# Output stores of 32 full rows, and a second product that takes its last inputs late in two of its four groups

## The chip, the cores and the metric

The kernel runs on one core of one Trainium2 chip. The metric is the device time of one execution in microseconds (us); the time of a kernel is the median of its runs.

## The reference

Three stages follow each other, all in float32 (the two feed-forward parts get their weights as float64 and convert them on the chip).

```python
# attention without softmax: q, k, v are 8 x 8 x 576 x 64 (batch, head, token, feature)
kv  = einsum('bhsd,bhse->bhde', k, v)
out = einsum('bhsd,bhde->bhse', q, kv)
out = out / sqrt(mean(out*out, axis=-1) + 1e-6) * g_norm
x   = out.transpose(0, 2, 1, 3).reshape(4608, 512)
# first feed-forward, 512 -> 768 -> 512
h = maximum(maximum(x @ w1, x @ w2), x @ w3)
x = h @ w_out
# second feed-forward, 512 -> 2048 -> 512
r = maximum(x @ w_in, 0)
y = (s * r*r + b) @ w_out2          # 4608 x 512
```

## The kernel before

Activations lie transposed, features on the 128 partitions and tokens along a row. Each float32 matrix product is made of three products of two halves (`mm3`: high by high, high by low, low by high); a half is split off by ScalarE (ACT, a rounding copy, line 91) and VectorE (DVE) or GpSimd (POOL, a subtraction, line 92).

**Order.** All steps are put on a list with a position (`at(pos, fn, ...)`) and traced in the order of their positions by `run`. TensorE (PE) and SyncE (SP, which issues every DMA of the kernel before) keep that order; DVE, ACT and POOL are ordered by a scheduler that works with estimated times, so their order can shift when an estimate does. A DMA waits, on SP, for its data, its buffer and the DMA eight places earlier in a rotation of eight semaphores; whatever stands behind it on SP waits too.

**Stage one, attention and first feed-forward** (to about 755 us). For each of nine token batches j, 18 groups `g1` (three weights by six blocks m of 128 hidden features) are computed while attention of the next batch is prepared. The maximum over three weights gives `h`, which `h_split` splits into a pair `h_m`. Then come four output groups `g2` (n = 0 to 3): `g2_mm` adds up 18 matmuls, three for each of `h_0` to `h_5`, in one PSUM bank; `g2_out` copies the bank and stores it to DRAM (`x1d`). In a batch after the first, group n stands at position t + 18 + n, its matmuls in the order m = 0 to 5.

**Stage two, input product of the second feed-forward** (about 755 to 1116 us), with a seven-product scheme (Winograd's) for 2 x 2 blocks.

**Stage three, output product** (about 1116 us to the end). Ten passes H = 0 to 9, two for each of five token groups; the last token group has half the width, so passes 8 and 9 take half the time. In each pass `z_load` brings operands from DRAM (`z<-gd`), `z_right` adds and splits them into six rotating `zx` pairs, `z_product` multiplies (product i of seven, four steps each, six matmuls a step), `z_combine` adds up on DVE. After each odd pass `put` turns the result: `o` is one of four rotating 128 x 512 buffers (`stage2`), DVE transposes 32 x 32 blocks into it (line 720), SP stores it. Buffer `o` number 5 can be written when the stores of number 1 have landed. In `o`, partition 32a + r at place (b, f) holds row 32b + r of 128 token rows, feature 128a + f. For pass pairs of full width there are eight `o` (32 stores of 64 KB, line 725), for the last pair four (32 stores of 32 KB, line 729). On SP the stores of a pair stand ahead of the `z_load`s of the pass after next; those for the next pass are out already, except for the last pass.

Of the kernel before, what the change touches and what calls it, by code (L numbers as in the profile page):

```python
# [8 lines left out]
F32 = mybir.dt.float32  # L9
F32R = mybir.dt.float32r  # L10
# [9 lines left out]
P = 128  # L20
N = 512
# [7 lines left out]
def attention_max_ffn_relu2_ffn(ctx: ExitStack, tc, q, k, v, g_norm, w1, w2, w3, wo, wi, w2o, s, b, out):  # L29
# [13 lines left out]
    nc = tc.nc  # L43
    B, H, S, D = q.shape
# [5 lines left out]
    M1 = DF1 // P  # L50
    M2 = DF2 // P
    REM = S - N
# [3 lines left out]
    G1 = 3 * M1  # L56
# [7 lines left out]
    def at(pos, fn, *args):  # L64
        plan.append((pos, len(plan), fn, args))
# [11 lines left out]
    base = ctx.enter_context(tc.tile_pool(name="base", bufs=1))  # L77
# [19 lines left out]
        nc.tensor.matmul(ps, lhsT=w[:, 1, sl], rhs=xh, start=False, stop=last)  # L97

    nc.scalar.preload_act_table_set("natural_log_exp_and_others")
    onesf = base.tile([P, P], F32, name="onesf")  # L100
    nc.vector.memset(onesf, 0.0)
    for h in range(2):
        nc.vector.memset(onesf[h * D:(h + 1) * D, h * D:(h + 1) * D], 1.0 / D)
    ones = base.tile([P, P], F32R, name="ones")
    nc.vector.tensor_copy(out=ones, in_=onesf)
    eps = base.tile([P, 1], F32, name="eps")
    nc.vector.memset(eps, EPS)
    g_sb = base.tile([P, 1], F32, name="g_sb")
# [17 lines left out]
    actx = ExitStack()  # L126
    at_ = actx.enter_context(tc.tile_pool(name="attn", bufs=1))
    psa = actx.enter_context(tc.tile_pool(name="psa", bufs=1, space=PSUM))

    kvf = at_.tile([P, NP, P], F32, name="kvf")  # L130
    nc.gpsimd.memset(kvf, 0.0)
# [172 lines left out]
    def o_sq(bb, p, src):  # L304
        sq = st["sq", p] = at_.tile([P, N], F32, tag="sq", name=f"sq_{bb}_{p}")
        act(out=sq, in_=src, func=AF.Square)
# [82 lines left out]
    def plan_kv(bb, load, mm):  # L389
        at(mm(0) - 2.9 * US, load_rem, bb)  # L390
        for p in range(NP):
            at(load(p), load_kv, bb, p)
            at(mm(p), kv_mm, bb, p)
        at(mm(NP - 1) + 1.2 * US, kv_out, bb)

    def plan_norm(bb, p, t, u):

        if bb:
            at(t + u, sq_split, bb, p)
        at(t + 3.3 * u, ms_mm, bb, p)  # L400
        at(t + 4 * u, ms_ln, bb, p)
        at(t + 6 * u, ms_newton, bb, p)
# [22 lines left out]
    for p in range(NP):  # L425
        a = 6.5 + 3.4 * p
# [15 lines left out]
    for j in range(NB):  # L442
        t = SL * j
        if j + 1 < B:
            bb = j + 1
            xpb = 3 if j else 2
            if bb < 4:
                kt = us(4 + 15 * bb)
                plan_kv(bb, lambda p: kt + (2 * p - 3.9) * US, lambda p: kt + 2 * p * US)
            else:  # L450
                plan_kv(bb, lambda p: t - 4 + p - 1.9, lambda p: t - 4 + p + 0.5)
            at(max(t - 10, us(20)), load_q, bb, 0, NP)
            at(t + 0.2, kv_diag, bb)
            for p in range(NP):
                a = t + 3 * p
                at(a + 0.4, q_turn, bb, p)
                if bb:
                    at(a + 1.3, q_split, bb, p)
                at(a + 3.5, o_mm, bb, p)
                at(a + 4.3, o_out, bb, p)  # L460
                plan_norm(bb, p, a + 4.5, 0.9)
                at(t + G1 + 0.2 + 0.5 * p, x_split, bb, p, nc.gpsimd if p < xpb else nc.vector)
            at(t + 13.3, o_rems, bb)
        elif j + 1 == B:
            for p in range(NP):
                a = t + 3 * p

                def sq(p=p):
                    st["o", B, p] = o_rem[:, p, :]
                    o_sq(B, p, o_rem[:, p, :])  # L470

                at(a + 0.4, sq)
                plan_norm(B, p, a + 0.5, 0.9)
                at(t + G1 + 0.2 + 0.5 * p, x_split, B, p, nc.gpsimd if p < 3 else nc.vector)
        for g in range(G1):
            if j or g >= 4:
                at(t + g, g1_part, j, g, range(KD))
            at(t + max(g, j == 0 and 3 or 0) + 1.01, g1_out, j, g)
            if g % 3 == 2:
                at(t + max(g, j == 0 and 3 or 0) + 1.25, h_split, j, g // 3)  # L480
        for n in range(KD):
            if j:
                at(t + G1 + max(n, 0.3), g2_mm, j, n, range(M1))
            at(t + G1 + n + 1.01 if j else t + G1 + 3 + 0.3 * n, g2_out, j, n)
        if not j:
            for m in range(M1):
                for n in range(KD):
                    at(t + G1 + 0.3 + m * 0.5 + 0.01 * n, g2_mm, j, n, [m])
# [12 lines left out]
    NQ = B // 2 + 1  # L501
# [23 lines left out]
    def stage2(nm):  # L525
        turn[0] += 1
        return base.tile([P, N], F32, tag=("t", "st")[turn[0] % 2], bufs=2, name=nm)
# [187 lines left out]
    def put(H, c, u):  # L715

        qq = H // 2
        o = stage2(f"o_{H}_{c}_{u}").rearrange("p (b f) -> p b f", b=4)
        for m in range(4):
            nc.vector.transpose(o[:, :, 32 * m:32 * m + 32], p2["o"][c][:, m, u * P:(u + 1) * P])  # L720
        for a in range(4):
            f, part = slice(a * P, (a + 1) * P), slice(32 * a, 32 * a + 32)
            if qq < NQ - 1:
                r0 = (2 * qq + c) * S + u * P
                nc.sync.dma_start(out=out[r0:r0 + P, f].rearrange("(b r) f -> r b f", r=32), in_=o[part])
            else:
                for e in range(2):
                    r0 = (4 * c + 2 * u + e) * S + N
                    nc.sync.dma_start(out=out[r0:r0 + REM, f].rearrange("(b r) f -> r b f", r=32),
                                      in_=o[part, 2 * e:2 * e + 2])  # L730

# [30 lines left out]
    for H in range(2 * NQ):  # L764
        t = T4 + 14 * H
        for i in range(7):
            for kk in range(4):
                at(t + 2 * i + 0.5 * kk - 2.4, z_right, H, i, kk)
                at(t + 2 * i + 0.5 * kk, z_product, H, i, kk)
            at(t + 2 * i + 1.9, z_combine, H, i)  # L770
        for i, free in ((0, 2), (1, 3), (4, 4), (5, 5), (6, 6)):
            for u in range(4 if i == 1 else 2):
                first = {0: -5.8, 1: (-3.8, -3.7, -1.8, 0.15)[u], 4: -4.8, 6: -3.8, 5: -2.8}[i]
                at(t + first if H == 0 else t - 14 + 2 * free - 2.4 + 1.55 + 0.01 * u, z_load, H, i, u)
        if H % 2:
            for c in range(2):
                for u in range(width(H // 2) // P):
                    at(t + 12.4 + 2 * c + 0.4 * u, put, H, c, u)
# [27 lines left out]
```

## Time and profile before

| | us |
|---|---|
| runs, median of 3 | 1494.72 (1493.74 to 1497.67) |
| profiled execution, time | 1489.72 |
| profiled execution, span | 1487.8 |
| TensorE busy (94%) | 1397.1 |
| VectorE busy (66%) | 985.7 |
| ScalarE busy (53%) | 784.2 |
| GpSimd busy (35%) | 524.9 |

The span is the profiled execution from its first to its last instruction. Busy shares are averages over three stages; waits are read stage by stage. PE's matmuls overlap, so the distance of two starts (0.23 us for 512 columns) is the measure of its pace and not the duration of one.

### The profile page before, as it was taken

To read this page: it belongs to the slowest core of one execution; us is meant where nothing else is said; L and a number is where in the kernel's file an instruction comes from. 1 tells how busy PE (TensorE), PEld (TensorE's weight loads), DVE (VectorE), ACT (ScalarE), POOL (GpSimd) and SP (SyncE) were. 2 spreads that over 40 slices of the span, in tenths; PEclk is the share of its full clock that TensorE was granted. 3 is DMA by queue.
4 is the path that set the end of the run, shared out by engine and by line. 5 is a ranking of instruction groups with operands and counts; after the bars stand their busy time and mean duration, and the time that the engine had idled before them with its cause. 6 is when DMAs were issued, how large, how long until landed. Compare 5 with 4: busy or idle time off the path is not lost.

```text
span 1487.8 us, 19756 instructions
## 1 busy us (share of the span) xinstructions
PE 1397.1 (94%) x6820; PEld 1143.4 (77%) x6820; DVE 985.7 (66%) x1561; ACT 784.2 (53%) x1393; POOL 524.9 (35%) x381
## 2 busy tenths in 40 slices
PE   5777899999999999999999999899998999999995
PEld 2565687878787878787878788887786888888895
DVE  4999564736363737354475746747887888988885
ACT  4545453535343535333366757766786555555553
POOL 3666443434353525331102223222433414141412
PEclk9889999999999999999999999999999999999998
DMA  9974242536374732313125344352667463646342
GB/s 199 196 192 82 85 74 92 104 127 104 107 110 120 111 108 56 86 36 113 46 106 204 138 165 165 124 194 114 219 225 243 127 201 114 214 136 178 120 133 66
DMA packets 232340, 198.44 MB, mean 133 GB/s; under 512 B 128176, under 2 KB 183472, under 8 KB 230576
## 3 DMA queue, kind: packets, MB, share of 16 engines
q1 hardware_dynamic: 232240, 197.19, 47.8%
q8 instruction: 53, 0.87, 0.3%
q14 instruction: 47, 0.39, 0.1%
HBM read 122.68 MB, written 74.45 MB: 133 GB/s over the span
## 4 chain that ended last, share of the span: by engine, by line
PE 36%; DVE 6%; issue 5%; DMA 4%; ACT 2%; POOL 2%; SPq 0%; DVEq 0%; POOLq 0%; ACTq 0%
PE zs_a L693 12%; PE ps_a L625 6%; PE zs_b L693 6%; PE zs_c L693 3%; PE ps_b L625 3%; PE g L96 1%; PE g L97 1%; PE g L95 1%; PE ps_c L625 1%; DVE cs L530 1%; DMA xl<-x1d 1%; DMA z<-gd 1%; DVE zx L92 1%; POOL d L530 1%; DVE x_q L92 1%
## 5 line engine op out<-in xcount | busy, mean ns | idle before, releaser
L95 PE MATMUL g<-xh,w_w 128*128 128x512 f32 x648 | 259.0, 403 | 5.4 <-ACT xh L91 5.4
L96 PE MATMUL g<-xl,w_w 128*128 128x512 f32 x648 | 258.7, 399 | 0.0
L97 PE MATMUL g<-xh,w_w 128*128 128x512 f32 x648 | 256.9, 397 | 0.0
L91 ACT ACTIVATE zx<-z 128x512 fp32r<-128x512 f32 (+1 forms) x280 | 162.0, 588 | 148.8 <-PE zs_a L693 56.3
L625 PE MATMUL ps_a<-x_q,w_q 128*128 128x512 f32 (+1 forms) x960 | 210.1, 370 | 11.3 <-DVE cs L530 8.4
L693 PE MATMUL zs_a<-zx,w_q 128*128 128x512 f32 (+1 forms) x960 | 203.2, 369 | 0.0
L625 PEld LDWEIGHTS ps_a<-x_q,w_q 128*128 128x128 f32 x960 | 167.4, 188 | 46.0 <-DVE cs L530 11.7
L92 DVE TENSOR_TENSOR zx<-z,zx 128x512 fp32r<-128x512 f32 (+1 forms) x234 | 172.2, 754 | 36.4 <-ACT zx L91 35.9
L693 PEld LDWEIGHTS zs_a<-zx,w_q 128*128 128x128 f32 x960 | 168.7, 189 | 30.4
L530 POOL TENSOR_TENSOR d<-cs,r 128x512 f32<-128x512 f32 (+1 forms) x40 | 59.8, 1503 | 282.7 <-ACT r L646 227.3
L95 PEld LDWEIGHTS g<-xh,w_w 128*128 128x128 f32 x648 | 123.7, 191 | 33.3 <-ACT xh L91 7.1
L97 PEld LDWEIGHTS g<-xh,w_w 128*128 128x128 f32 x648 | 124.4, 192 | 27.9 <-issue 0.5
L96 PEld LDWEIGHTS g<-xl,w_w 128*128 128x128 f32 x648 | 124.5, 192 | 26.5 <-DVE xl L92 0.4
L92 POOL TENSOR_TENSOR zx<-z,zx 128x512 fp32r<-128x512 f32 (+1 forms) x46 | 60.0, 1303 | 210.8 <-ACT zx L91 210.8
L167 POOL TENSOR_TENSOR tr_ctr<-tr_ctr 128x512 int32<-128x512 int32 x42 | 55.9, 1330 | 191.1 <-ACT tr_ctr L160 186.8
L369 DVE TENSOR_TENSOR h<-g,h 128x512 f32<-128x512 f32 x108 | 73.9, 684 | 57.7 <-PE g L97 57.6
L693 PE MATMUL zs_b<-zx,w_q 128*128 128x512 f32 (+1 forms) x480 | 105.6, 374 | 5.2 <-DVE zx L92 4.5
L625 PE MATMUL ps_b<-x_q,w_q 128*128 128x512 f32 (+1 forms) x480 | 105.5, 368 | 0.6 <-ACT cs L635 0.5
L693 PEld LDWEIGHTS zs_b<-zx,w_q 128*128 128x128 f32 x480 | 84.6, 191 | 23.0 <-DVE zx L92 6.8
L625 PEld LDWEIGHTS ps_b<-x_q,w_q 128*128 128x128 f32 x480 | 84.2, 188 | 16.1 <-ACT cs L635 1.0
L96 PE MATMUL g<-h,w_o 128*128 128x512 f32 x216 | 85.6, 396 | 10.1 <-DVE h L92 10.1
L95 PE MATMUL g<-h,w_o 128*128 128x512 f32 x216 | 86.5, 400 | 6.3 <-ACT w_o L91 4.2
(156 smaller groups left out, 2433.4 us busy)
## 6 DMA issues: line engine op xcount, KB each, us to landing
z<-gd SPq DMA_DIRECT2D x64, 512.0 KB, 4.4
gd<-cs SPq DMA_DIRECT2D x96, 256.0 KB, 2.0
z<-gd SPq DMA_DIRECT2D x48, 256.0 KB, 4.1
x1d<-x SPq DMA_DIRECT2D x36, 256.0 KB, 2.8
k<-in_k_dram SPq DMA_DIRECT2D x32, 256.0 KB, 4.7
v<-in_v_dram SPq DMA_DIRECT2D x32, 256.0 KB, 5.1
raw_craw<-in_moe_w_in_dram SPq DMA_DIRECT2D x16, 512.0 KB, 4.2
wd<-tr_ctr SPq DMA_DIRECT2D x32, 256.0 KB, 2.9
```

The costliest lines, as they stand in the source:

```text
L91: act(out=hi, in_=src, func=AF.Copy)
L92: eng.tensor_tensor(out=lo, in0=src, in1=hi.bitcast(F32), op=ALU.subtract)
L95: nc.tensor.matmul(ps, lhsT=w[:, 0, sl], rhs=xh, start=first, stop=False)
L96: nc.tensor.matmul(ps, lhsT=w[:, 0, sl], rhs=xl, start=False, stop=False)
L97: nc.tensor.matmul(ps, lhsT=w[:, 1, sl], rhs=xh, start=False, stop=last)
L167: nc.gpsimd.tensor_tensor(out=t, in0=t, in1=r, op=ALU.add)
L369: nc.vector.tensor_tensor(out=st["h", m], in0=ps, in1=st["h", m], op=ALU.max)
L530: eng.tensor_tensor(out=out, in0=in0, in1=in1, op=op)
L625: nc.tensor.matmul(ps, lhsT=w[:, a, c], rhs=x[:, b_, :n], start=new and k == 0 and e == 0, stop=k == HK - 1 and e == 2, skip_group_check=True)
L693: nc.tensor.matmul(ps, lhsT=w[:, a, c], rhs=x[:, b_, :n], start=new and k_ == 0 and e == 0, stop=k_ == 3 and e == 2, skip_group_check=True)
```

## The change

**The stores.** A store now takes one place b of `o`: 32 token rows with all 512 features, from all 128 partitions, to one closed piece of 64 KB in DRAM. The DRAM side is written as 4 feature blocks of 32 rows of 128 features, the SBUF side as 128 partitions of 128 features. Number and size stay the same for the full-width pairs (32 of 64 KB); the last pair has 16 of 64 KB where it had 32 of 32 KB, and four of these, those with odd j of the second half c = 1, are issued by ACT.

**The second product.** In batches 1 to 8, groups n = 0 and n = 1 first take `h_0` to `h_4`, and then both take `h_5`; groups 2 and 3 are as before. `g2_out` of group 0 moves from position 1.01 to 2.01 after the start of the groups, that of group 1 from 2.01 to 2.11.

**Constants.** `onesf` and `ones` move from the pool that lasts to the pool of the attention stage.

```diff
         for n in range(KD):
             if j:
-                at(t + G1 + max(n, 0.3), g2_mm, j, n, range(M1))
-            at(t + G1 + n + 1.01 if j else t + G1 + 3 + 0.3 * n, g2_out, j, n)
+                if n < 2:
+                    at(t + G1 + max(n, 0.3), g2_mm, j, n, range(M1 - 1))
+                    at(t + G1 + 1.8 + 0.01 * n, g2_mm, j, n, [M1 - 1])
+                else:
+                    at(t + G1 + n, g2_mm, j, n, range(M1))
+            at(t + G1 + max(n + 1.01, 2.01 + 0.1 * n) if j else t + G1 + 3 + 0.3 * n, g2_out, j, n)
...
-        for a in range(4):
-            f, part = slice(a * P, (a + 1) * P), slice(32 * a, 32 * a + 32)
+        for j in range(4):
             if qq < NQ - 1:
-                r0 = (2 * qq + c) * S + u * P
-                nc.sync.dma_start(out=out[r0:r0 + P, f].rearrange("(b r) f -> r b f", r=32), in_=o[part])
+                r0 = (2 * qq + c) * S + u * P + 32 * j
             else:
-                for e in range(2):
-                    r0 = (4 * c + 2 * u + e) * S + N
-                    nc.sync.dma_start(out=out[r0:r0 + REM, f].rearrange("(b r) f -> r b f", r=32),
-                                      in_=o[part, 2 * e:2 * e + 2])
+                r0 = (4 * c + 2 * u + j // 2) * S + N + 32 * (j % 2)
+            eng = nc.scalar if qq == NQ - 1 and c and j % 2 else nc.sync
+            eng.dma_start(out=out[r0:r0 + 32].rearrange("r (a f) -> a r f", a=4), in_=o[:, j])
```

On PE, where the second product of batch 1 begins (`g_1_0` and `g_1_1` are its first two groups), the order before is:

```order
L95 MATMUL g_1_0_1821<-h_4_1757,w_o_1185 128x512
L96 MATMUL g_1_0_1821<-h_4_1757,w_o_1185 128x512
L97 MATMUL g_1_0_1821<-h_4_1757,w_o_1185 128x512
L95 MATMUL g_1_0_1821<-h_5_1818,w_o_1237 128x512
L96 MATMUL g_1_0_1821<-h_5_1818,w_o_1237 128x512
L97 MATMUL g_1_0_1821<-h_5_1818,w_o_1237 128x512
L95 MATMUL g_1_1_1845<-h_0_1438,w_o_1007 128x512
```

Now the rows with `h_5` of the first group stand behind 15 matmuls of the second:

```order
L97 MATMUL g_1_1_1842<-h_4_1757,w_o_1185 128x512
L95 MATMUL g_1_0_1821<-h_5_1818,w_o_1237 128x512
L96 MATMUL g_1_0_1821<-h_5_1818,w_o_1237 128x512
L97 MATMUL g_1_0_1821<-h_5_1818,w_o_1237 128x512
L95 MATMUL g_1_1_1842<-h_5_1818,w_o_1237 128x512
L96 MATMUL g_1_1_1842<-h_5_1818,w_o_1237 128x512
L97 MATMUL g_1_1_1842<-h_5_1818,w_o_1237 128x512
```

Both groups end later by that, and the third begins at the same place as before.

On DVE, in the first steps of pass 8 (`o_1_1` to `o_1_3` are the sixth to eighth `o` of the pair before it), the order before is:

```order
L720 STREAM_TRANSPOSE o_1_1_12205<-xlo_11552 128x4x32 x4
L530 TENSOR_TENSOR z_2_11955<-z_2_11955,z_0_1_11903 128x256
L530 TENSOR_TENSOR z_3_11957<-z_3_11957,z_0_1_11903 128x256
L530 TENSOR_TENSOR z_0_11951<-z_0_11951,z_5_0_12043 128x256
L530 TENSOR_TENSOR z_1_11953<-z_1_11953,z_5_0_12043 128x256
L720 STREAM_TRANSPOSE o_1_2_12223<-xlo_11552 128x4x32 x4
L92 TENSOR_TENSOR zx_12276<-z_2_11955,zx_12276 128x256
L92 TENSOR_TENSOR zx_12286<-z_3_11957,zx_12286 128x256
L720 STREAM_TRANSPOSE o_1_3_12238<-xlo_11552 128x4x32 x4
```

Now more of pass 8's own work stands between the last two `o`:

```order
L724 STREAM_TRANSPOSE o_1_2_12223<-xlo_11552 128x4x32 x4
L92 TENSOR_TENSOR zx_12314<-z_1_11953,zx_12314 128x256
L534 TENSOR_TENSOR z_3_11957<-z_3_11957,z_5_1_12045 128x256
L92 TENSOR_TENSOR zx_12324<-z_2_11955,zx_12324 128x256
L92 TENSOR_TENSOR zx_12351<-z_4_0_12001,zx_12351 128x256
L92 TENSOR_TENSOR zx_12364<-z_4_0_12001,zx_12364 128x256
L92 TENSOR_TENSOR zx_12373<-z_4_1_12003,zx_12373 128x256
L724 STREAM_TRANSPOSE o_1_3_12238<-xlo_11552 128x4x32 x4
```

The transposes moved back by about five DVE instructions; after the earlier pairs they moved back by two to four.

On SP, at the end of the program, before:

```order
L670 DMA z_6_1_12473<-gd_97 128x2x256
L729 DMA out_dram<-o_0_0_12781 32x2x128 x8
L729 DMA out_dram<-o_0_1_12800 32x2x128 x8
L729 DMA out_dram<-o_1_0_12827 32x2x128 x8
L729 DMA out_dram<-o_1_1_12840 32x2x128 x8
```

and now, with two more of each of the last two on ACT:

```order
L674 DMA z_6_1_12473<-gd_91 128x2x256
L731 DMA out_dram<-o_0_0_12781 4x32x128 x4
L731 DMA out_dram<-o_0_1_12796 4x32x128 x4
L731 DMA out_dram<-o_1_0_12819 4x32x128 x2
L731 DMA out_dram<-o_1_1_12828 4x32x128 x2
```

The shape is that of the DRAM side, its outermost size first: 32 before, 4 now. 32 issues on SP became 12, and 4 on ACT.

## Rows read from the trace of the kernel before

**Rows 1.** Waits of PE over the span: total us, times, longest us
```profile
PE g L96 <- DVE h L92: 10.1, 7, 2.4
```

**Rows 2.** Stretches: us, busy (count) of PE, PEld, DVE, ACT, POOL; PEclk, DMA share, GB/s
```profile
200.00:752.00 552.00, 541.91 (x2647) 442.08 (x2646) 294.20 (x430) 231.61 (x402) 204.22 (x144) 1.00 0.39 93
...
1196.00:1221.00 25.00, 25.00 (x112) 20.71 (x111) 24.62 (x56) 14.53 (x25) 4.19 (x3) 1.00 0.59 167
1221.00:1233.00 12.00, 12.00 (x55) 9.93 (x54) 7.16 (x11) 5.45 (x10) 1.98 (x2) 1.00 0.78 253
...
1428.00:1444.00 16.00, 15.87 (x121) 15.08 (x120) 14.40 (x49) 9.30 (x26) 3.31 (x4) 1.00 0.50 127
1445.00:1451.00 6.00, 6.00 (x52) 6.00 (x52) 4.18 (x12) 3.58 (x9) 0.74 (x1) 1.00 0.84 238
```

**Rows 3.** PE in order of time, batches 1 and 2: start us, us, line, tile [idle before]
```profile
225.91 0.39 PE L95 MATMUL g<-h,w_o 128*128 128x512 f32 x1
227.45 0.50 PE L96 MATMUL g<-h,w_o 128*128 128x512 f32 x1 [1.15 <-DVE h L92]
228.02 0.39 PE L95 MATMUL g<-h,w_o 128*128 128x512 f32 x1
228.71 0.39 PE L95 MATMUL g<-h,w_o 128*128 128x512 f32 x1
...
301.22 0.50 PE L96 MATMUL g<-h,w_o 128*128 128x512 f32 x1 [2.39 <-DVE h L92]
```

**Rows 4.** SP in order of time, behind pass 7 and at the end
```profile
1428.03 16.71 SPq L725 DMA_DIRECT2D out_dram<-o  x32
1444.84 0.94 SPq L670 DMA_DIRECT2D z<-gd  x2
...
1470.57 14.90 SPq L729 DMA_DIRECT2D out_dram<-o  x32
```

**Rows 5.** First split of pass 9 on ACT and DVE, and PE at its start
```profile
1447.82 0.42 ACT L91 ACTIVATE zx<-z 128x256 fp32r<-128x256 f32 x1 [0.29 <-PE zs_c L693]
1448.30 5.92 PE L693 MATMUL zs_a<-zx,w_q 128*128 128x256 f32 x48
1448.48 0.42 DVE L92 TENSOR_TENSOR zx<-z,zx 128x256 fp32r<-128x256 f32 x1
```

**Rows 6.** Stores, full-width pairs and last: issue ns min/median/max; landing of the last's
```profile
L725 SPq DMA_DIRECT2D out_dram<-o x128: 315/444/2125, 1199.8 to 1443.2; - x128
...
L729 SPq DMA_DIRECT2D out_dram<-o x32: 343/425/427, 1470.6 to 1485.0; - x32
...
DMA to landing us min/median/max: 1.5/1.6/1.6
```

**Rows 7.** Issues of weight loads with unequal sides (512 pieces onto 128 partitions of 4)
```profile
L146 SPq DMA_DIRECT2D raw_craw<-in_moe_w_out_dram x68: 328/622/2239, 102.2 to 637.5; - x68
```

**Rows 8.** DMA of 1475 to 1485 us: packets, share of 16 engines, issues
```profile
DMA packets 1681, 0.69 MB, mean 69 GB/s; under 512 B 337, under 2 KB 1681, under 8 KB 1681
...
q1 hardware_dynamic: 1681, 0.69, 26.8%
...
out_dram<-o SPq DMA_DIRECT2D x22, 32.0 KB, 1.6
```

**Rows 9.** DVE in order of time, behind the stores of the first pair
```profile
1203.85 0.68 DVE L530 TENSOR_TENSOR z<-z,z 128x512 f32<-128x512 f32 x1
1204.45 0.88 DVE L720 STREAM_TRANSPOSE o<-xlo 128x128 f32<-128x128 f32 x4
1205.25 0.65 DVE L92 TENSOR_TENSOR zx<-z,zx 128x512 fp32r<-128x512 f32 x1
```

**Rows 10.** PE after an idle stretch, and two stretches behind it (columns as in rows 2)
```profile
1129.31 1.96 PE L693 MATMUL zs_b<-zx,w_q 128*128 128x512 f32 x5 [3.50 <-DVE zx L92]
...
1130.00:1136.00 6.00, 5.37 (x14) 3.68 (x13) 4.67 (x8) 2.89 (x6) 0.00 (x0) 0.50 0.49 131
1137.00:1143.00 6.00, 6.00 (x28) 4.95 (x27) 2.68 (x4) 3.94 (x7) 1.36 (x2) 1.00 0.59 175
```

More of the change, by code (lines that the diff above doesn't have):

```diff
@@ L99, in attention_max_ffn_relu2_ffn @@
     nc.scalar.preload_act_table_set("natural_log_exp_and_others")
[L100 to L105, printed above, removed]
     eps = base.tile([P, 1], F32, name="eps")
@@ L128, in attention_max_ffn_relu2_ffn @@
     psa = actx.enter_context(tc.tile_pool(name="psa", bufs=1, space=PSUM))
+    onesf = at_.tile([P, P], F32, name="onesf")
+    nc.vector.memset(onesf, 0.0)
+    for h in range(2):
+        nc.vector.memset(onesf[h * D:(h + 1) * D, h * D:(h + 1) * D], 1.0 / D)
+    ones = at_.tile([P, P], F32R, name="ones")
+    nc.vector.tensor_copy(out=ones, in_=onesf)
     kvf = at_.tile([P, NP, P], F32, name="kvf")
```

## The prediction

> **What bounds the kernel now.** I first read the waits of PE over the whole span, since PE is busy for 94% of it. One is regular: the low half of the last `h` in the second product, seven times, 10.1 us in all [rows 1]. From 200 to 752 us PE is idle for 552.00 - 541.91 = 10.1 us, which is all of it [rows 2]: time won there is won for the end. PE's order of time shows one such place in each of batches 1 to 7, of 1.15 us in batch 1 and of 2.39, the longest, in batch 2 [rows 3]. In stage three PE has hardly a gap, but two neighbours run close behind it. Behind a pair's stores DVE is busy for 24.62 of 25 us [rows 2]. Behind pass 7 the loads for pass 9 leave SP only when 32 stores are out, at 1444.84, and pass 9 begins on PE at 1448.30 + 2.9 = 1451.2 (half of the 48 matmuls are pass 8's last) [rows 4, 5]. At the end the bound is SP: 32 issues take 14.90 us from 1470.57, the last starts at 1485.05 and lands 1.6 us later, at 1486.6 [rows 4, 6].
>
> **The second product.** A triple of matmuls has a pitch of 0.69 us (228.02 to 228.71). The triple on `h_5` takes 2.11 us in batch 1 (225.91 to 228.02), 1.42 too many, where the gap alone is 1.15 [rows 3]; with 0.27 more at each of seven places the 10.1 become 12.0. The 15 matmuls now ahead of `h_5` take 5 x 0.69 = 3.4 us, and `h_5` is never later than 2.39 + 0.3, so all of it is covered; the matmuls are the same in number. Late next would be the inputs of the following batch, for which no wait stands in this stretch. I take **-12.0** (-10.1, the bare gaps, to -12.0). The copies and stores of groups 0 and 1 leave later, and on SP behind loads of keys and values; what they write is read only in stage two. The moved constants are the same few DVE instructions at the start. These cost nothing.
>
> **Issue of the stores.** Sides of unequal shape are found in the weight loads: 622 ns an issue against 444 for a store now [rows 6, 7]. With 0.05 us between two, a burst of 32 holds SP for 32 x 0.67 = 21.4 us instead of 16.7 [rows 4], if nothing else does.
>
> **How many engines a store uses.** All DMAs of this kernel have outermost sizes that 16 divides on both sides (32, 64, 128 or 512), and each leaves about 16 packets under 512 B: 337 for 22 stores, of which one falls partly outside the stretch [rows 8]. I read that as 16 engines for each. The new DRAM side has 4 as its outermost size and the SBUF side 128. If a DMA is cut along its outermost sizes, only 4 equal cuts fit both, and a store runs on four engines. No row shows such a DMA. But no row needs a cut along an inner size either, and without one four is the answer; I hold it for likelier by about five to one. The Trainium skill, page "DMA: Bandwidth & Descriptors", section "Why a DMA increments its semaphore by 16 and not by 1", says that a DMA from SP takes as many engines as the largest number up to 16 that divides the slowest sizes of both sides: four here, the sum below, and not the -16.6 of sixteen. By that rule the stores of now take 16, and the trace agrees with its 16 small packets.
>
> Price of four: the last stores give 69 GB/s at 26.8% of 16 engines, 16.1 GB/s an engine, so that 65.5 KB on four take 1.02 us [rows 8]; the burst behind pass 7 (127 GB/s at 0.50) 1.03; stretches with longer pieces 0.93 (238 GB/s at 0.84) and 0.81 (253 at 0.78) [rows 2]. The first two are stores in the same pieces of 512 B, but with sixteen engines writing at once and four to eight times the small packets for each byte; four engines should disturb each other less. I take **0.92**, between the ends 0.81 and 1.03. Store number n of a burst then lands 1.7 + 0.92 n after the first issue (1.7: the 1.6 of now and 0.2 more issue, less its own packets).
>
> **Behind passes 1, 3 and 5.** Buffers of `o` come free later, and DVE waits. First pair: stores start at 1199.8 [rows 6], sets of four land at 1205.2, 1208.9, 1212.5 and 1216.2. DVE's instructions have a pitch of 0.60, four transposes one of 0.80 [rows 9]. In the new order the fifth `o` is due at 1205.05, the sixth four instructions after it, the seventh three and a slow split later, the eighth four later: waits of about 0.15, 0.5, 1.0 and 0.5, 2.2 us. The splits of the pass queue behind them on DVE, and PE waits for those; but the six `zx` pairs are a stock. Nothing to 2.2 us a burst reaches PE; I take 0.7, three times: **+2.1** (0 to 6.6). The loads behind these bursts are for the next pass, which is a full one away; the burst grows by some 13 us, and I give that no price.
>
> **Behind pass 7.** Here the passes are half as long, and this place decides. The loads for pass 9 stand behind 32 stores on SP and, on the four engines, behind their packets: 1428.03 + 1.7 + 32 x 0.92 = 1459.2; own transfer of 256 KB at 283 GB/s (238 / 0.84) 0.9; ACT, DVE and hand-over 1.2 (1447.8 to 1448.9 now, and 0.1). PE can begin pass 9 at 1461.3 instead of 1451.2, **+10.1** [rows 2, 4, 5]. DVE's waits in pass 8 lie inside that. After 3.50 us of idling PE had its clock at 0.50, 1.2 GHz, for at least 6 us, and at 1.00 by 1137 [rows 10]: up to 3 us of work lost, some of it beside DVE's own backlog: **+2.0** (0 to 3).
>
> **The end.** 12 issues on SP take 8 us and four on ACT run beside them, so the engines decide: 16 stores have landed 1.7 + 16 x 0.92 = 16.4 us after 1470.57; now it is 16.0. **+0.4** (-1.4 to +2.2). What SP saves in issues, four engines take back. The section "Issuing engines are not separate DMA queues" of the same page of the Trainium skill says that DMAs of different issuing engines run on the same 16 DMA engines and that a second issuer saves issue time only; no run here shows a second queue, and without it the sum is the same.
>
> **Sum.** -12.0 + 2.1 + 10.1 + 2.0 + 0.4 = +2.6 us. The profiled execution took 1489.72, so 1492.3; the runs' median is 5.0 above it, 1494.72, and with the same +2.6 the forecast is **1497.3**. All times below are on the median's scale.
>
> **Rivals.** *Slower.* The same stores at 1.03 us, the price of their own rows. From about 0.95 us on the eighth `o` comes so late that DVE's waits (4 us a burst) outrun the stock of `zx`: 6.6 for three bursts; pass 9 at 1428.03 + 1.7 + 33.0 + 2.1 = 1464.8, 13.6 late; clock 2.5; end 2.2; with -12.0 it is +12.9, **1508**. For it: the rows are the same kind of packet. Against it: they were sixteen abreast. *Quick packets.* At 0.81 us: bursts 0.5, pass 9 6.5 late, clock 1.7, end -1.4, in all -4.7, **1490**. *Sixteen engines after all.* Then issue is the bound. The loads for pass 9 start 4.6 us later, of which PE has 2.3 in hand (the first split is ready at 1448.9 and used at 1451.2), so 2.3; at the end the last issue starts at 1477.9 and lands at 1479.7 instead of 1486.6, -6.9; with -12.0 it is -16.6, **1478**. For it: no row shows fewer engines.
>
> **How the numbers follow.** Forecast (0.92; sums from -2 to about +5) 0.45; slower 0.28; quick 0.10; sixteen engines 0.17. A measurement of this kernel can tell about 0.3%, 4.5 us, from no change. Faster: sixteen 0.17 and half of quick, 0.22. Slower: 0.28 and an edge of the forecast, 0.31. Same: the rest, 0.47. The range takes in forecast, quick and nearly all of slower, 8 in 10: 1488 to 1510; sixteen is left out. The forecast's own range is 1493 to 1500.
>
> **What would show it.** Right: no wait for `h` on PE in batches 1 to 7, and stage two 12 us earlier; stores that leave 4 small packets instead of 16 and whose landings follow each other by about 0.9 us; a gap of some 10 us on PE ahead of pass 9 with the loads `z<-gd` as its cause, and a clock of 0.50 behind it; from the end of PE to the last landing the same time as now. Wrong: landings 0.67 us apart and an end 7 us shorter (sixteen engines); DVE waits of 4 us and more behind passes 1, 3 and 5 that PE repeats (slower); a new wait in the second product.

## The result and the profile after

The changed kernel takes **1481.0 us** (median of 4, 1480.2 to 1482.6), the kernel before 1494.2 (median of 4). The ratio is 0.9916, with an interval of 0.9897 to 0.9936, so it is faster by about 13 us. The forecast was 1497.3 with a range from 1488 to 1510. It missed: both the sign and the range are wrong.

The profiled executions stand closer together. The changed one took 1480.35 us with a span of 1478.6, the one before 1489.72 with 1487.8. The difference in span is **-9.2 us**, and only this can be followed step by step.

**Stage one.** The stretch of rows 2 that had 10.1 us of idle time has none now (stretch: us, busy of PE, PEld, DVE, ACT, POOL, PEclk, DMA share, GB/s):

```profile
200.00:740.00 540.00, 540.00 (x2653) 443.76 (x2652) 294.35 (x434) 233.40 (x407) 205.47 (x144) 1.00 0.39 95
```

The wait of rows 1 for `h` is gone. In PE's order the second product of batch 1 begins and ends here (`g<-h` begins it, `g<-xh` is the next batch's first product):

```profile
221.49 0.39 PE L95 MATMUL g<-h,w_o 128*128 128x512 f32 x1
...
237.81 0.39 PE L95 MATMUL g<-xh,w_w 128*128 128x512 f32 x1
```

That is 16.32 us. In the kernel before it began at 222.51 and ended at 240.27, which is 17.76. Read in the same way, batches 1 to 7 won 1.44, 2.66, 1.43, 1.44, 1.44, 1.47 and 2.24, in all 12.1 us.

**Pass 9.** SP in order of time, behind pass 7 and at the end; it answers to rows 4:

```profile
1413.00 22.70 SPq L731 DMA_DIRECT2D out_dram<-o  x32
1435.81 1.11 SPq L674 DMA_DIRECT2D z<-gd  x2
...
1462.48 10.59 SPq L731 DMA_DIRECT2D out_dram<-o  x12
```

And the chain of waits at the start of pass 9 (start us, us, what):

```profile
1435.81 4.38 DMA z<-gd
1440.23 0.04 issue
1440.28 0.42 ACT zx L91
1440.74 5.67 PE zs_a L697 x24
1446.41 2.88 PE zs_b L697 x24
```

The load needs 4.38 us from issue to landing, ACT waits for it, and PE waits for ACT. In the kernel before, the load at this place (issued at 1444.84) needed 2.9 us (last column):

```profile
z<-gd SPq DMA_DIRECT2D x1, 256.0 KB, 2.9
```

Among PE's waits this one is new (total us, times, longest):

```profile
PE zs_a L697 <- ACT zx L91: 3.6, 1, 3.6
```

The first 24 matmuls of pass 9 run from 1440.74 to 1446.25, 5.51 us, where 24 take 2.88 at full clock. The clock shows why (columns as above):

```profile
1441.00:1446.00 5.00, 5.00 (x23) 4.83 (x24) 4.49 (x12) 2.71 (x8) 0.73 (x1) 0.50 0.99 329
```

**The stores.** Packets, and their time as a share of 16 engines, while the burst behind pass 7 runs (1416 to 1436 us), answering to rows 8:

```profile
DMA packets 3422, 1.72 MB, mean 86 GB/s; under 512 B 102, under 2 KB 3421, under 8 KB 3421
q1 hardware_dynamic: 3421, 1.70, 28.5%
```

By the trace's semaphore events the 32 stores land one behind the other, the first at 1415.48, the last at 1439.49. That is 0.775 us for each (24.01 / 31). In these 20 us about 26 stores leave 102 small packets, 4 for each, where a store left 16 before. The semaphores count the same: that of a new store is raised once soon after its issue and four times as the data land, that of an old store sixteen times.

**Issue or engines.** A new store also takes SP longer to issue than an old one, 537 ns against 444, so the issues could have been what makes the load late. The first ten new stores leave SP 0.60 us apart (1413.00 to 1418.39), the others 0.76 us apart (1418.97 to 1435.01), which is the pace of the landings. At 0.60 us all through, the first load would leave SP 19.2 us after the first store instead of 22.8; behind the old stores it left after 16.8. Counted from the first store, that load landed at 19.7 us before (at 1447.72) and lands at 27.2 us now (at 1440.19), which is 7.5 us later. Before, pass 9 began 3.46 us after that landing, now it begins 0.55 us after it, so that PE had 2.9 us in hand and 4.6 us are left. By this estimate the longer issues alone are 2.4 us, less than PE had in hand; the four engines make the gap.

**The end.** From the first of the last stores to the last landing it takes 14.9 us (1462.48 to 1477.41); before, 16.0.

### The profile page after: what moved, and what is told of

Same layout as the page of the kernel before. It is cut to its first block, busy times and chain, and to the rows that moved or that the text cites. A ratio compares the mean times of both kernels' runs of the same rounds, so it can differ in the third digit from the quotient of the medians.

```text
span 1478.6 us, 19743 instructions
## 1 busy us (share of the span) xinstructions
PE 1397.7 (95%) x6820; PEld 1147.4 (78%) x6820; DVE 984.8 (67%) x1561; ACT 783.9 (53%) x1393; POOL 527.5 (36%) x381
## 4 chain that ended last, share of the span: by engine, by line
PE 74%; DVE 9%; issue 5%; DMA 4%; ACT 2%; SPq 2%; POOL 2%; DVEq 0%; ACTq 0%; POOLq 0%
PE g L95 12%; PE g L97 12%; PE g L96 12%; PE zs_a L697 12%; PE ps_a L629 8%; PE zs_b L697 6%; PE ps_b L629 4%; PE zs_c L697 3%; PE ps_c L629 2%; SPq L271 1%; DVE cs L534 1%; PE kvps L240 1%; DMA gd<-r 1%; DMA raw_o<-in_moe_w_dram 1%; DVE zx L92 1%
## 5 line engine op out<-in xcount | busy, mean ns | idle before, releaser
L697 PE MATMUL zs_a<-zx,w_q 128*128 128x512 f32 (+1 forms) x960 | 206.4, 373 | 3.7 <-ACT zx L91 3.6
L95 PEld LDWEIGHTS g<-xh,w_w 128*128 128x128 f32 x648 | 123.7, 191 | 31.1 <-ACT xh L91 5.5
L95 PE MATMUL g<-h,w_o 128*128 128x512 f32 x216 | 86.2, 399 | 6.3 <-ACT w_o L91 4.2
L92 POOL TENSOR_TENSOR h<-h,h 128x512 fp32r<-128x512 f32 x40 | 59.3, 1482 | 82.8 <-ACT h L91 82.7
```

The source lines that it names most:

```text
L92: eng.tensor_tensor(out=lo, in0=src, in1=hi.bitcast(F32), op=ALU.subtract)
L95: nc.tensor.matmul(ps, lhsT=w[:, 0, sl], rhs=xh, start=first, stop=False)
L697: nc.tensor.matmul(ps, lhsT=w[:, a, c], rhs=x[:, b_, :n], start=new and k_ == 0 and e == 0, stop=k_ == 3 and e == 2, skip_group_check=True)
```

## Experiments

In the table, "half clock" is the time with a granted clock of 0.50 between 200 and 1105 us, that is, behind the start and ahead of stage three. "End" runs from the first of the last pair's stores to the last landing. Each ratio is against runs of the kernel before that were taken together with those of the row, so it can differ a little from the quotient of the medians in the table.

| kernel | median us | ratio to before | span us | half clock us | gap ahead of pass 9 us | end us |
|---|---|---|---|---|---|---|
| before | 1494.2 | 1 | 1487.8 | 0 | 0 | 16.0 |
| after | 1481.0 | 0.9916 (0.9897 to 0.9936) | 1478.6 | 0 | 3.6 | 14.9 |
| g2_only | 1480.3 | 0.9909 (0.9880 to 0.9938) | 1478.5 | 6.8 | 0 | 16.0 |
| stores_only | 1498.5 | 1.0027 (1.0010 to 1.0045) | 1497.3 | 10.2 | 3.6 | 14.8 |
| old_full_new_end | 1475.8 | 0.9883 (0.9854 to 0.9913) | 1476.8 | 6.8 | 0 | 15.1 |
| delay | 1476.9 | 0.9890 (0.9861 to 0.9919) | 1477.1 | 13.7 | 0 | 14.7 |
| sp_only | 1481.4 | 0.9909 (0.9881 to 0.9937) | 1479.7 | 0 | 3.6 | 14.2 |
| end_two | 1494.1 (one run) | | 1492.3 | 6.8 | 3.6 | 26.8 |
| end_mixed | 1475.8 | 0.9874 (0.9848 to 0.9899) | 1477.0 | 13.7 | 0 | 13.6 |
| before_again | 1491.7 | 0.9997 (0.9975 to 1.0020) | 1488.2 | 0 | 0 | 16.0 |
| after_again | 1481.4 | 0.9918 (0.9893 to 0.9944) | 1485.4 | 10.2 | 3.6 | 15.4 |
| consts_g2 | 1478.4 | 0.9900 (0.9866 to 0.9933) | 1475.8 | 3.4 | 0 | 16.0 |

My theory was that the gain is the second product's, and that the new stores cost time behind pass 7, since a store runs on four engines and the loads for pass 9 stand behind 32 of them. Each run below takes one part of that away or doubles it.

### The second product alone (g2_only)

The kernel before, with this change of its step list only:

```diff
-                at(t + G1 + max(n, 0.3), g2_mm, j, n, range(M1))
+                if n < 2:
+                    at(t + G1 + max(n, 0.3), g2_mm, j, n, range(M1 - 1))
+                    at(t + G1 + 1.8 + 0.01 * n, g2_mm, j, n, [M1 - 1])
+                else:
+                    at(t + G1 + n, g2_mm, j, n, range(M1))
-            at(t + G1 + n + 1.01 if j else t + G1 + 3 + 0.3 * n, g2_out, j, n)
+            at(t + G1 + max(n + 1.01, 2.01 + 0.1 * n) if j else t + G1 + 3 + 0.3 * n, g2_out, j, n)
```

> The kernel before with the new order of the second product alone; stores and constants as before. Accounting of the changed kernel by batches: in the second products themselves PE won 12.1 us (batches 1 to 7: 1.44, 2.66, 1.43, 1.44, 1.44, 1.47, 2.24), and another 3.1 us elsewhere ahead of stage three (0.7 in the first 141 us, about 1.4 in the first products, 1.0 in stage two). Theory A: the 3.1 us belong to the order too; span 15 us below that of the kernel before, 1472.6, and pass 9 begins without a gap. Theory B: only the 12.1 us belong to it, and the rest is scatter of one execution or comes from the moved constants; span 1475.7. Both: no wait for h longer than 0.3 us in batches 1 to 7.

The span was 1478.5, and the ratio 0.9909. Two stretches at half clock lie in its stage two, 6.8 us in all; they cost up to 3.4 us of PE. Without them the span is about 1475, near theory B. So the order of the second product is worth some 12 us. Its median (1480.3) is about the changed kernel's (1481.0), though by the terms of the last table the changed kernel should be some 4.5 us slower; a few runs scatter by as much. The profiles do show the difference: without the half-clock stretches, and with the first second product as early as in the changed kernel (141.59 instead of 142.77), the span here would be about 1473.9 against 1478.6. The first products still take 54.91 us a batch here, so the 0.19 us that the changed kernel saves on each is not the order's.

### The stores alone (stores_only)

The changed kernel with the old list of steps for the second product (the diff above, undone).

> The changed kernel with the old order of the second product: new stores and moved constants alone. Theory A (four engines for a store, its price 0.775 us as read behind pass 7 of the changed kernel): loads for pass 9 land about 4.7 us too late, PE idles about 3.6 us ahead of pass 9 and works at half the clock behind it (2.8 us more), the end is 1.2 us shorter: span about 6.3 us above the kernel before, 1494.1. Rival: the gap ahead of pass 9 comes from the shift of stage two, not from the stores; then no gap, and the span is 1.2 us below, 1486.6.

The span was 1497.3, of which three stretches at half clock (10.2 us) account for up to 5.1; the 1492.2 that are left are near theory A's 1494.1 and not the rival's 1486.6. The ratio, 1.0027, lies above 1 with its whole interval: the new stores, even with the moved constants, make the kernel slower. SP and PE in order of time at pass 9:

```profile
1432.01 22.53 SPq L727 DMA_DIRECT2D out_dram<-o  x32
...
1459.60 5.65 PE L693 MATMUL zs_a<-zx,w_q 128*128 128x256 f32 x24 [3.59 <-ACT zx L91]
```

Pass 9 begins 27.6 us after the first store. Before, it was 23.15 (1428.03 to 1451.18), in the changed kernel 27.7. So the gap comes with the stores, wherever stage two ends.

### Old stores behind the passes, new ones at the end (old_full_new_end)

```diff
...
+        if qq < NQ - 1:
+            for a in range(4):
+                f, part = slice(a * P, (a + 1) * P), slice(32 * a, 32 * a + 32)
+                r0 = (2 * qq + c) * S + u * P
+                nc.sync.dma_start(out=out[r0:r0 + P, f].rearrange("(b r) f -> r b f", r=32), in_=o[part])
+            return
...
```

> The changed kernel with the old stores (32 partitions of one feature block, 128 rows) behind passes 1, 3, 5 and 7 and the new ones for the last pair. Theory A: the loads for pass 9 stand behind 32 issues of 0.52 us again instead of 24.8 us of four engines' packets; no gap ahead of pass 9, clock 1.00, the end as short as in the changed kernel: 7.5 us below the changed kernel, span 1471.1. Rival (the gap has another cause, such as the order of the second product): span as the changed kernel, 1478.6, with the gap of 3.6 us.

SP and PE, behind pass 7 and at pass 9:

```profile
1418.02 17.32 SPq L729 DMA_DIRECT2D out_dram<-o  x32
1435.44 0.93 SPq L674 DMA_DIRECT2D z<-gd  x2
...
1438.30 5.92 PE L697 MATMUL zs_a<-zx,w_q 128*128 128x256 f32 x48
```

The gap is gone: 48 matmuls run through in 5.92 us, at full clock. Pass 9 begins at 1438.30 + 2.88 = 1441.18, 23.16 us after the first store, as before. The span of 1476.8 missed the 1471.1. The 6.8 us at half clock in stage two cost up to 3.4 of these 5.7 us, and the first second product began 1.6 us later than in the changed kernel (143.23 instead of 141.59). By the medians the version is 5 us faster than the changed kernel (1475.8 against 1481.0): its four runs took 1474.4 to 1478.6, those of the changed kernel 1480.2 to 1482.6, though the intervals of the two ratios overlap a little.

### The same stores, half of them later (delay)

Nothing is taken away here. The 16 stores of the second half of the pair are only issued behind the loads `z_0` to `z_5` of pass 9:

```diff
...
+        p2["put", H, c, u] = o
+        if not (H == 7 and c):
+            put_store(H, c, u)
+
+    def put_store(H, c, u):
+        qq, o = H // 2, p2["put", H, c, u]
...
                     at(t + 12.4 + 2 * c + 0.4 * u, put, H, c, u)
+                    if H == 7 and c:
+                        at(T4 + 126 - 3 + 0.01 * u, put_store, H, c, u)
```

> The changed kernel, but the last 16 of the 32 stores behind pass 7 are issued behind the loads z_0 to z_5 of pass 9; the transposes stay where they are. Nothing is removed. Theory A (the loads are late because of the stores ahead of them): z_0 for pass 9 lands by about 1431, no gap ahead of pass 9, span about 7 us below the changed kernel, 1471.5; the last store of the pair lands by about 1448, ahead of those of the end. Rival (PE waits because DVE and ACT are behind through the late buffers of o): the gap of 3 to 4 us stays, span 1478.

SP and then PE in order of time:

```profile
1418.03 10.37 SPq L736 DMA_DIRECT2D out_dram<-o  x16
1428.51 1.11 SPq L674 DMA_DIRECT2D z<-gd  x2
1429.71 3.09 SPq L671 DMA_DIRECT2D z<-gd  x4
1432.90 4.08 SPq L674 DMA_DIRECT2D z<-gd  x4
1437.03 11.97 SPq L736 DMA_DIRECT2D out_dram<-o  x16
...
1430.58 1.70 PE L697 MATMUL zs_b<-zx,w_q 128*128 128x256 f32 x12 [0.36 <-DVE zx L92]
...
1438.97 5.92 PE L697 MATMUL zs_a<-zx,w_q 128*128 128x256 f32 x48
```

The loads leave at 1428.51, and PE goes from pass 8 into pass 9 without a gap. The first load lands at 1433.8, later than the 1431 expected, and the last store of the pair at 1452.9, not 1448, but still ahead of the end. Pass 9 begins 23.8 us after the first store, 0.7 later than before. That rest is the small gaps in pass 8 (0.36 of them in the row above). Such a gap stands in every profile with the new stores behind pass 7 and in none with the old ones. DVE waits 1.5 us for buffers of `o` there; that its order was also shifted (see the change) wasn't tried apart. So the rival holds for 0.7 us and the order on SP for the other 3.9 of the 4.6 us. The predicted span of 1471.5 was missed again, at 1477.1, with 13.7 us at half clock, which cost up to 6.8.

### One queue instead of two (sp_only)

```diff
-            eng = nc.scalar if qq == NQ - 1 and c and j % 2 else nc.sync
-            eng.dma_start(out=out[r0:r0 + 32].rearrange("r (a f) -> a r f", a=4), in_=o[:, j])
+            nc.sync.dma_start(out=out[r0:r0 + 32].rearrange("r (a f) -> a r f", a=4), in_=o[:, j])
```

> The changed kernel with all 16 last stores issued by SP, none by ACT. In the changed kernel the last store landed 14.9 us after the first issue (1462.48 to 1477.41). Theory A (the four engines are the end's bound, 0.775 us for a store; the second queue buys nothing): 16 issues of 0.6 us fit beside them, 14.9 us within 0.5. Rival (the second queue runs four stores beside SP's): 4 x 0.775 = 3.1 us more, 18.0 us.

From the first issue to the last landing it took 14.2 us, a little below theory A's 14.4 to 15.4 and far from the rival's 18.0; the changed kernel took 14.9 (15.4 in its second profile). SP's 16 issues:

```profile
1464.31 10.78 SPq L730 DMA_DIRECT2D out_dram<-o  x16
```

Sixteen issues end after 10.78 us, and the last store lands 3.5 us later. The second queue buys nothing, since issue isn't the bound. The section "Issuing engines are not separate DMA queues" of the Trainium skill (page "DMA: Bandwidth & Descriptors") says that a second issuing engine saves only the time of issuing, and the run agrees.

### Stores on two engines (end_two)

For the last pair alone:

```diff
-            eng.dma_start(out=out[r0:r0 + 32].rearrange("r (a f) -> a r f", a=4), in_=o[:, j])
+            for h in range(1 if qq < NQ - 1 else 2):
+                k = 4 if qq < NQ - 1 else 2
+                eng.dma_start(out=out[r0:r0 + 32, 256 * h:256 * h + P * k].rearrange("r (a f) -> a r f", a=k),
+                              in_=o[64 * h:64 * h + 32 * k, j])
```

> The changed kernel with each of the last 16 stores cut in two, 64 partitions each (2 feature blocks, 32 KB), so that the outermost size of the DRAM side is 2. Theory A (a store is cut into as many parts as its outermost sizes allow, and the same two engines serve all): 2 small packets left by each store, and 32 stores at 0.775 us with 1.7 ahead, 26.5 us from first issue to last landing instead of 14.9. Rival 1 (as before 4 engines or more for a store): bound by SP's 24 issues of 0.6 us, about 16.5 us. Rival 2 (two engines, but other ones for the two halves): 16.5 us also, with 2 small packets each.

The end took 26.8 us, against 26.5 by theory A. Packets from 1470 to 1490 us:

```profile
DMA packets 1705, 0.85 MB, mean 42 GB/s; under 512 B 51, under 2 KB 1705, under 8 KB 1705
q1 hardware_dynamic: 1181, 0.59, 9.8%
q10 hardware_dynamic: 524, 0.26, 4.5%
```

At 0.775 us a store, 20 us hold 26 of them, which left 51 small packets: 2 for each. Each semaphore is raised twice as the data land. The rate is half that of the changed kernel's burst, 42 GB/s instead of 86. So a store ran on as many engines as its outermost DRAM size, and all stores ran on the same ones. The Trainium skill has the number of engines as a rule, the largest number up to 16 that divides the slowest sizes of both sides (page "DMA: Bandwidth & Descriptors", section "Why a DMA increments its semaphore by 16 and not by 1"), and four and two both agree with it. The price of an engine's share is the same with two engines as with four, so between these two numbers it isn't made by the engines disturbing each other.

### Old and new stores at the end (end_mixed)

As old_full_new_end; in the last pair the third `o` goes out in 8 old stores on ACT, and the fourth in 8 old ones on SP.

```diff
...
+        old = qq < NQ - 1 or c
...
+                for e in range(2):
+                    r0 = (4 * c + 2 * u + e) * S + N
+                    (nc.sync if u else nc.scalar).dma_start(
+                        out=out[r0:r0 + REM, f].rearrange("(b r) f -> r b f", r=32), in_=o[part, 2 * e:2 * e + 2])
...
```

> A version from the findings: new order of the second product and moved constants; old stores behind passes 1, 3, 5 and 7; at the end the first two o in 8 new stores on SP, the third in 8 old stores of 32 KB on ACT, the fourth in 8 old ones on SP. Theory A (the end of the changed kernel is bound by four engines, that of the kernel before by SP's issues; sharing out both wins): last landing about 10 us after the first issue instead of 14.9; time about 5 us below that of the kernel with old stores and the new end (1475.8), near 1471. Rival (writes of 1 MB at the end are bound by something shared): 13 to 15 us, no gain.

The end took 13.6 us and not 10. What SP waited for there (total us, times, longest; L738 issues the new stores, L734 the old):

```profile
SPq L734 <- DMA out_dram<-o: 2.5, 4, 0.9
SPq L738 <- DMA out_dram<-o: 1.8, 1, 1.8
```

SP stood for 4.3 us, since each DMA waits for the one eight places earlier, and those ran slowly on four engines. I had left that rotation out. The median is that of old_full_new_end, 1475.8.

### Both kernels again (before_again, after_again)

The two programs, unchanged, to see what separates their executions.

> The kernel before once more. Its first profiled execution took 1489.72 us, 5 us below its median, and had no stretch at a granted clock of 0.50 in stage two; executions of other kernels here show two to four such stretches of 3.4 us there (near 819, 945 and 1025 us), each worth 1.7 us of PE. Theory A (these stretches are the scatter of the times): an execution near the median of 1495 shows about three of them, and the span without their 1.7 us each is again 1487 to 1489. Rival (the 5 us are elsewhere, in the first 140 us or in DMA): a clock of 1.00 in stage two at a time near the median.

> The changed kernel once more; first profiled execution 1480.35 us, 0.7 below its median, no stretch at 0.50 in stage two. Theory A: an execution without such stretches takes 1480 to 1481 again, and one with n of them 1.7 n more. Rival: the median stays near 1481 although the profile shows such stretches.

The profiled execution of the kernel before took 1490.14 us, again without a stretch at half clock, while other executions of it reached 1498.2. That of the changed kernel took 1487.22, 6 us more than its median, and it shows three such stretches in stage two (columns as above):

```profile
926.00:932.00 6.00, 5.77 (x35) 5.62 (x35) 1.73 (x5) 3.26 (x10) 2.85 (x4) 0.72 0.26 93
947.00:952.00 5.00, 4.38 (x17) 3.86 (x18) 5.00 (x12) 4.35 (x10) 0.00 (x0) 0.66 0.15 52
1066.00:1072.00 6.00, 4.91 (x14) 3.87 (x15) 6.00 (x11) 3.05 (x5) 0.00 (x0) 0.72 0.37 145
```

They cost (1 - 0.72) x 6, (1 - 0.66) x 5 and (1 - 0.72) x 6, which is 1.7 us each and 5.1 in all. Another 2.1 us were lost by the start of the first second product (143.67 instead of 141.59). Together that is 7.2, where the span grew by 6.8. So the scatter of the changed kernel is understood to half a microsecond. For the kernel before no trace shows it, as both of its profiles happen to have none of these stretches. But every execution has its mean granted clock on record. In 45 runs of the kernel before, the 12 below 1490.5 us (1489.2 in the mean) had a clock of 0.9796, the 18 above 1494.5 us (1496.6) one of 0.9744. That is 7.7 us of clock over the span for 7.4 us of time: its scatter, too, goes with the clock, though not even this tells at which places.

### The place of the constants (consts_g2)

The changed kernel with the old stores everywhere; against g2_only it moves `onesf` and `ones` alone.

> The changed kernel with the old stores everywhere: new order of the second product and moved constants. In the first products a batch took 54.91 us with the constants in their old place (kernel before, and new order alone) and 54.72 with them in the new one (changed kernel, new stores alone). Theory A (the place of the constants is worth 0.19 us a batch): 54.72 in batches 2 to 7, and 1.4 us less in stage one than with the new order alone. Rival (it comes with the stores, or from the order of DVE): 54.91. Both: no gap ahead of pass 9; the end as in the kernel before, 16 us from first issue to last landing.

The first products of batch 3, from their first matmul (`g<-xh`) to the first of the second product (`g<-h`). First g2_only, then consts_g2:

```profile
389.38 0.50 PE L95 MATMUL g<-xh,w_w 128*128 128x512 f32 x1
...
444.29 0.39 PE L95 MATMUL g<-h,w_o 128*128 128x512 f32 x1
```

```profile
389.39 0.50 PE L95 MATMUL g<-xh,w_w 128*128 128x512 f32 x1
...
444.11 0.39 PE L95 MATMUL g<-h,w_o 128*128 128x512 f32 x1
```

54.91 us became 54.72, with the same matmuls in the same order, and theory A holds. The time is lost right behind the matmuls that use `ones` as weights, in four places of the batch, with 0.04 to 0.05 us at each. PE at the first of them, three starts behind, in g2_only and then in consts_g2:

```profile
413.64 0.40 PE L95 MATMUL g<-xh,w_w 128*128 128x512 f32 x1
413.87 0.40 PE L96 MATMUL g<-xl,w_w 128*128 128x512 f32 x1
414.11 0.39 PE L97 MATMUL g<-xh,w_w 128*128 128x512 f32 x1
```

```profile
413.65 0.39 PE L95 MATMUL g<-xh,w_w 128*128 128x512 f32 x1
413.87 0.39 PE L96 MATMUL g<-xl,w_w 128*128 128x512 f32 x1
414.10 0.39 PE L97 MATMUL g<-xh,w_w 128*128 128x512 f32 x1
```

The pitch is 0.23 to 0.24 us in g2_only, and 0.227 in consts_g2. Seven batches make 1.3 us, of the 1.4 that all first products of the changed kernel won. The move also shifts the addresses of the tiles that last; which of the two it is wasn't tried, and why an address should matter stays open.

## Why the prediction was wrong

**What was right.** The second product: -12.0 predicted, -12.1 measured in the batches, with no new wait. Four engines for a store, against the sixteen of a rival. The place that decides: loads for pass 9 behind the stores, with a clock of 0.50 behind the gap. The clock's price: +2.0 predicted, +2.6 measured (5.51 - 2.88).

**The step that failed: the price of a store on four engines.** I took 0.92 us for each store of 64 KB, and it is 0.775, below even the lower end of 0.81. I had divided GB/s by the DMA share of 16 engines. In the burst of the changed kernel the same division gives 86 / (0.285 x 16) = 18.9 GB/s, or 0.87 us for 16.4 KB. But the rate itself says 65.5 KB / 86 = 0.76, and the landings say 0.775. The share shows what is wrong: 0.285 x 16 is 4.6 engines, where four were at work. In end_two it is 0.143 x 16 = 2.3 for two. The times of packets on one engine overlap: in the burst of the changed kernel 4 to 8 packets are open at any moment, never fewer than 4, and in end_two 2 to 4. So the share counts them too high by about 15%, and a rate divided by it comes out too low. All four prices that I had were made in this way. This is 0.10 of the 0.15 us (0.87 to 0.775); the other 0.05 (0.92 to 0.87) is the choice between the four. The reason that I gave for that choice (sixteen engines at once disturb each other) pointed the right way: a packet of 512 B took 31.6 ns in the mean in the old burst behind pass 7 (1429 to 1444 us), and 27.5 in the new one (1422 to 1434 us). Between four and two engines it played no part.

What hung on the price:

| term | predicted us | measured us |
|---|---|---|
| second product | -12.0 | -12.1 |
| constants | 0 | -1.4 |
| bursts behind passes 1, 3, 5 | +2.1 | 0 |
| pass 9 begins later | +10.1 | +4.6 |
| clock behind it | +2.0 | +2.6 |
| the end | +0.4 | -1.3 |
| not in the sum: the first 140 us, stage two | | -1.6 |
| sum | +2.6 | -9.2 |

*Pass 9.* The last store landed 26.5 us after the first issue, as 1.7 + 32 x 0.775 says, and not 31.1. That is 4.6 of the 5.5 us. The other 0.9 is the hand-over, for which I had 2.1 us; from the last landing to PE it took 1.25 (1439.49 to 1440.74). By the quick rival's own steps the price measured gives pass 9 about 5.4 us late. The price of an issue, 0.67 us, was too high as well (0.60 for the first ten stores), but the sum didn't hang on it.

*Bursts.* PE has no gap above 0.25 us in passes 2 to 7, and from the first store behind pass 1 to the first behind pass 7 it takes 228.20 us (1184.80 to 1413.00), where it took 228.23 before (1199.80 to 1428.03). DVE's waits for a buffer of `o` are 1.6 us over all four bursts, where I had 2.2 for each (waits of DVE from 1170 to 1450 us: total us, times, longest):

```profile
DVE o L724 <- DMA out_dram<-o: 1.6, 4, 0.8
```

*The end.* From the end of PE's last matmul to the end of the span it took 16.2 us before and 14.9 now. The price of 0.775 alone would give 1.9 less; sp_only came closest to that.

**A second error: "these cost nothing".** The moved constants are few instructions, but the move, by their own place in memory or by the shift of the others', is worth about 1.4 us on PE. I had looked only at the instructions that move.

**A third: the scale.** I added the 5.0 us between the profiled execution of the kernel before and its median to the forecast. The changed kernel's profiled execution lay only 0.7 below its median, so that medians moved by 13.2 us where the spans moved by 9.2. The 1.6 us of the last term are of the same kind. The first second product began anywhere between 141.6 and 143.9 us in the profiles here. The profiled execution of the kernel before was a lucky one, with a clock of 0.980; by the clocks on record (see before_again) its slower ones had a lower clock, by about as much as they were slower. Even so, -9.2 on the median would have been 1485.5, below the range.

The rival "quick packets" (1490) had the right mechanism and nearly the right price. But the price was near by luck: 0.81 was made by the same division, which counts 15% too much, from rows with longer pieces, and the two errors went against each other.

## What to carry to other kernels

Take the rate of a few engines from bytes and landings, not from GB/s divided by a busy share: such a share counted packets' times 15% too high here. In these runs a store's outermost DRAM size set how many engines shared it (32: sixteen; 4: four; 2: two), so ask of every store with a small outermost size what is queued behind it; moving 16 of 32 stores behind the next loads took the whole gap away. A gain at one place and a loss at another can hide each other in one time; the version that keeps the gain and leaves out the loss (old stores behind the passes) was the faster one by its runs.

## What was unexpected

The clock fell to 0.50 for a few us in stage two, in some executions and not in others of the same program. No such fall was seen in either profile of the kernel before, three in the second one of the changed kernel, four stretches' worth (13.7 us) in delay and end_mixed. Each follows one or two gaps of PE of 0.6 to 2 us, and nearly the same gaps stand in the profiles without a fall. At 1.7 us each, these are as large as the terms that were argued over.

With two 128 x 128 constants in another place, the pitch of a few matmuls behind those that use them went from 0.23 and 0.24 to 0.227 us, without any wait that the profile records.

A second issuing queue made the end no shorter: 14.7 to 15.4 us in five profiles with four stores on ACT, 14.2 in the one with all on SP. SP waited for stores there (waits of SP behind 1462 us in the changed kernel: total us, times, longest),

```profile
SPq L731 <- DMA out_dram<-o: 3.5, 3, 1.6
```

two of the three times for a store that ACT had issued eight places earlier in the rotation and that landed late (at 1469.57 and 1471.89). The medians, 1481.0 and 1481.4, don't show a difference.
